# Reordering the first and the last stage of a one-core attention block kernel: load order, parking, interleaved broadcasts, double-buffered weights and row sums on two engines

## The chip, the cores and the metric

The kernel runs on one core of a Trainium2 chip. The metric is the device time of one execution in microseconds (us); the lower, the better. Runs of the kernel before, on the same chip, go with every group of runs, because the chips differ by a little over 0.1% for one and the same kernel.

In the profile PE is TensorE (matmul), DVE is VectorE, ACT is ScalarE, POOL is GpSimd, SP is SyncE. A load or store lands when its last bytes have been moved. The granted clock is the share of TensorE's full clock that the profile shows as granted. A line such as `1800.43 8.15 DVE L642 TENSOR_TENSOR wq_sb<-wq_sb,bc_t 128x15360 ...` reads: start in us, busy us, engine, source line, operation, output and inputs, their shapes, how many are put together (x2), and in square brackets how long the engine stood idle before it and what released it.

## The reference, cut to what matters

A decode step of a transformer block whose normalisation is modulated by a conditioning vector `c`; the kernel returns the output and the gradients of nine inputs.

```python
mod = (silu(c) @ w_mod).reshape(1, 6, 1, 640)          # w_mod: 640 x 3840
sa, ca, ga, sb, cb, gb = mod[:, 0], ..., mod[:, 5]
h = layernorm(x) * (1 + ca) + sa                       # 1 x 640
q = h @ wq                                             # wq: 640 x 6144, 32 heads of 192
o = softmax(q k^T * 192 ** -0.5) v                     # k, v cache: 32 heads x 8192 x 192
x = x + ga * (o @ wo)
...                                                    # MLP, modulated by sb, cb, gb
# outputs: x, and by the chain rule d_x, d_k, d_v, d_wq, d_wo, ..., d_c, d_w_mod
```

What matters for the tail, given the gradient `dq` (6144 numbers): `d_wq = h^T dq` (an outer product, 640 x 6144), `d_h = dq @ wq^T` (row sums of `wq * dq`), and from `d_h` the gradient `d_mod` (3840 numbers); then `d_w_mod = silu(c)^T d_mod` and `d_silu = d_mod @ w_mod^T` in the same two forms.

## The kernel before: the parts that the change touches

Helpers: `row_to_col` turns a row on one partition into columns, by one small fp32 matmul for each 128 elements; `park` keeps such columns in memory for the end; `col_to_row` and `unpark` turn them back, also by matmuls and copies by ACT; `vecmat` multiplies a column vector with a weight matrix in chunks of 512; `bcast_row` spreads a row over 128 partitions by a matmul with ones and a copy.

The head, before the first key block is used:

```python
    x0 = load_row(A_x[0], D, "x0")
    c_row = load_row(c, D, "c_row")
    # ... silu(c) -> sc, sc_col_f, sc_col_bf
    wmod_sb = w0.tile([P, NDC, NMOD], BF16, name="wmod_sb")
    nc.sync.dma_start(out=wmod_sb, in_=w_mod.rearrange("(i p) n -> p i n", p=P))
    wq_sb = w0.tile([P, NDC, QD], BF16, name="wq_sb")
    nc.gpsimd.dma_start(out=wq_sb, in_=A_wq.rearrange("(i p) n -> p i n", p=P))

    vecmat(sc_col_bf, NDC, wmod_sb, NMOD, mod_row, chunk=480)
    # ... layernorm -> n0; h_a -> ha_col_f, ha_col_bf
    vecmat(ha_col_bf, NDC, wq_sb, QD, qs_row_bf, chunk=512, scale=SCALE)
    bcast_row(qs_row_bf, QD, qs_bc, copy_eng="scalar")
    x0_c = park(x0, NDC, "x0_c")
    c_c = park(c_row, NDC, "c_c")
    sig_c = park(sig, NDC, "sig_c")
    mod_c = park(mod_row[0:1, D : 6 * D], 5 * NDC, "mod_c")
    n0_c = park(n0, NDC, "n0_c")
```

Then come the forward attention, the output projection and the MLP with their gradients, and the backward attention, which ends with `dq_col_f`. None of this changes. The tail:

```python
    nc.vector.tensor_copy(out=dq_col_f, in_=dqcol_ps)
    # ...
        wmod_sb2 = fin.tile([P, NDC, NMOD], BF16, name="wmod_sb2")
        nc.sync.dma_start(out=wmod_sb2, in_=w_mod.rearrange("(i p) n -> p i n", p=P))
        col_to_row(dq_col_f, NQC, dq_row_bf)                       # all 48 columns
        for half in range(2):
            hs = slice(half * QH, (half + 1) * QH)
            wq_sb2 = fin.tile([P, NDC, QH], BF16, name="wq_sb2", tag="wqh")   # one buffer
            nc.sync.dma_start(out=wq_sb2, in_=wq_v[:, :, hs])
            # ... dq_bc = this half of dq, on all partitions
            nc.vector.tensor_tensor(out=wq_sb2, in0=wq_sb2, in1=dq_bc[:, None, :].to_broadcast([P, NDC, QH]), op=ALU.mult)
            # dha_c, or dha_c2 and a sum for half 1:
            nc.vector.reduce_sum(out=dha_c, in_=wq_sb2, axis=AX.X)
            for i in range(NDC):                                   # staged outer product, two buffers
                stg = fino.tile([P, NMOD], BF16, name="stg", tag="stg")
                nc.vector.tensor_scalar(out=stg[:, 0:QH], in0=dq_bc, scalar1=ha_col_f[:, i : i + 1], scalar2=None, op0=ALU.mult)
                nc.gpsimd.dma_start(out=out_4[i * P : (i + 1) * P, hs], in_=stg[:, 0:QH])
        d_ha = unpark(dha_c, NDC, "d_ha")
        n0 = unpark(n0_c, NDC, "n0r")
        # ... car, d_x1, sig, c_row, and four col_to_row into d_mod: nine steps in all
        # ... d_mod complete, layernorm backward, d_x
        # ... dmod_bc = d_mod on all partitions, in one go
        nc.vector.tensor_tensor(out=wmod_sb2, in0=wmod_sb2, in1=dmod_bc[:, None, :].to_broadcast([P, NDC, NMOD]), op=ALU.mult)
        nc.vector.reduce_sum(out=dsc_c, in_=wmod_sb2, axis=AX.X)
        # ... five staged outer products into out_9; unpark(dsc_c); d_c; store
```

## Time and profile before

| what | kernel before |
|---|---|
| time, median of the first 4 runs (lowest to highest) | 1945.89 us (1944.86 to 1947.25) |
| modulation weights landed, first product on PE | 30.21 us |
| query products start | 58.07 us |
| first K product on DVE | 79.67 us |
| copy of dq_col | 1753.06 us |
| last dK store landed | 1768.0 us |
| end of the span | 1944.0 us |

The windows view of the kernel before, one line a stage: head, forward attention, MLP and projections, backward attention, tail. After the length come the busy us of each engine with its instructions in brackets, then the granted TensorE clock, the busy share of the DMA engines, and what they moved.

```profile
core 0: us, PE busy (x) PEld busy (x) DVE busy (x) ACT busy (x) POOL busy (x), PEclk, DMA share, GB/s
0.00:80.00 80.00, 50.24 (x222) 30.13 (x222) 6.64 (x21) 25.20 (x44) 2.13 (x10) 0.86 0.49 199
80.00:640.00 560.00, 289.41 (x2339) 238.17 (x2340) 451.99 (x354) 224.16 (x1186) 2.22 (x1) 0.69 0.93 369
640.00:815.00 175.00, 98.12 (x485) 54.26 (x483) 67.08 (x141) 39.84 (x80) 19.48 (x26) 0.64 0.63 181
815.00:1753.00 938.00, 279.81 (x2176) 226.27 (x2176) 882.20 (x2492) 688.86 (x2013) 67.14 (x126) 0.63 0.99 420
1753.00:1944.00 191.00, 40.48 (x226) 20.60 (x226) 105.49 (x38) 27.67 (x60) 10.96 (x19) 0.58 0.41 163
```

The two attention stages have the DMA engines busy for 93% and 99% of the time (in the second, DVE is busy for 882 of 938 us too). The change takes no work out of them; it is meant to let them start earlier, and e1 below tests whether they hand that on. In the head (first line) and the tail (last line) no engine is near 100%: there one thing waits for the next, and these 271 us are what the change works on.

The timeline of PE in the head of the kernel before:

```profile
30.21 9.98 PE L173 MATMUL vm_ps<-wmod_sb,sc_col_bf 128*1 128x480 bf16 x40 [20.92 <-DMA wmod_sb<-in_w_mod_dram]
...
45.21 10.80 PE L161 MATMUL col_ps<-ones_row_f,mod_row 1*128 1x1 f32 x50
55.87 2.27 PE L161 MATMUL col_ps<-ones_row_f,ln_n 1*128 1x1 f32 x10
58.07 14.55 PE L173 MATMUL vm_ps<-wq_sb,ha_col_bf 128*1 128x512 bf16 x60
```

and of DVE, the first K product:

```profile
79.67 6.63 DVE L320 TENSOR_TENSOR prod<-K_sb,qs_bc 128x6144 bf16<-128x6144 bf16 x2 [21.33 <-PE bc_ps L150]
```

PE stands idle for 20.92 us until the modulation weights are there. Then 10.80 us of parking stand ahead of the query products, although in the source the parks are written after them: what is written last need not run last. The products are followed by twelve broadcasts, and the first key product on DVE comes at 79.67.

The chain of waits at the start of the tail of the kernel before (start, us, what):

```profile
1754.06 13.95 DMA out_dram<-dK
1768.46 0.58 ACT dq_row_bf L120
1769.09 11.54 PE c2r_ps L118 x80
```

The last dK store takes 13.95 us to land; only then does the chain go on, because the memory of the tail's tiles is the one that the stores still read. Then 48 columns are turned to rows (11.54 us) before the first broadcast.

The timeline of DVE in the same tail:

```profile
1784.31 1.95 DVE L651 TENSOR_SCALAR stg<-bc_t,ha_col_f 128x3072 bf16<-128x3072 bf16 x2 [31.04 <-ACT bc_t L152]
1794.52 1.02 DVE L651 TENSOR_SCALAR stg<-bc_t,ha_col_f 128x3072 bf16<-128x3072 bf16 x1 [8.26 <-DMA out_dram<-stg]
...
1800.43 8.15 DVE L642 TENSOR_TENSOR wq_sb<-wq_sb,bc_t 128x15360 bf16<-128x15360 bf16 x1
1808.62 16.15 DVE L644 TENSOR_REDUCE dha_c<-wq_sb 128x5 f32<-128x15360 bf16 x1
...
1835.82 1.02 DVE L651 TENSOR_SCALAR stg<-bc_t,ha_col_f 128x3072 bf16<-128x3072 bf16 x1 [9.19 <-DMA out_dram<-stg]
...
1844.06 8.15 DVE L642 TENSOR_TENSOR wq_sb<-wq_sb,bc_t 128x15360 bf16<-128x15360 bf16 x1
1852.25 16.16 DVE L647 TENSOR_REDUCE dha_c<-wq_sb 128x5 f32<-128x15360 bf16 x1
...
1906.00 20.15 DVE L678 TENSOR_REDUCE dsc_c<-wmod_sb 128x5 f32<-128x19200 bf16 x1
```

All five staged products run ahead of each multiply, and with two buffers the third waits until the first has been stored (8.26 and 9.19 us). A reduction takes twice as long as the multiply before it. The waits view sums the waits for staged stores up (engine and line, waited for what, us in all, times, longest):

```profile
DVE stg L651 <- DMA out_dram<-stg: 25.7, 6, 9.2
DVE stg L681 <- DMA out_dram<-stg: 2.9, 2, 1.8
```

That is 28.6 us in 8 waits. Not all of it lengthens the chain: with one buffer the load of the second half is issued 71.7 us after the dq_col copy and lands at 88.1, so the second multiply, at 91.0, could have come at most 2.9 us earlier without any wait for a store.

### The profile page before, as it was taken

Reading aid. Unit: us, or ns where it says so; the run is one execution under the profiler, and the core shown is the slowest. Engines: PE = TensorE matmul, PEld = TensorE weight load, DVE = VectorE, ACT = ScalarE, POOL = GpSimd, SP = SyncE. Lnnn points to the kernel's source line nnn. Section 1 sums busy time; section 2 is a strip of 40 time slices with the busy share of each in tenths; the row PEclk is TensorE's granted clock in tenths of the full one; section 3 lists DMA queues with packets and bytes.
Section 4 is the critical chain, followed back from the end, with each engine's and each line's share of the span. In section 5 each row is a group of like instructions: output and inputs, shape, how many; then the busy total and the mean of one; then the engine's idle time right before and its main releaser. Section 6 shows DMA issues by size and latency. Waiting matters only on the chain. (4 is left out here: it accounts for less than half of the span.)

```text
span 1944.0 us, 18733 instructions
## 1 busy us (share of the span) xinstructions
PE 758.0 (39%) x5447; PEld 569.4 (29%) x5447; DVE 1513.4 (78%) x3043; ACT 1005.7 (52%) x3379; POOL 101.9 (5%) x181
## 2 busy tenths in 40 slices
PE   4644555555554754433223233232232232333030
PEld 2333444444444433222222122122122121232010
DVE  1268888888888153499899999999999999991667
ACT  2424434444344211576677777776776777782020
POOL 0000000000000011100000000000000000010000
PEclk9667777676677755666566566666665666666565
DMA  6599999999996528999999999999999999979402
GB/s 263 198 402 417 377 379 372 381 372 379 383 380 271 139 65 204 343 385 429 429 429 429 428 427 429 429 429 429 429 428 427 424 426 427 426 314 370 194 5 101
DMA packets 112621, 678.93 MB, mean 349 GB/s; under 512 B 53764, under 2 KB 53767, under 8 KB 62727
## 3 DMA queue, kind: packets, MB, share of 16 engines
q1 hardware_dynamic: 86278, 432.17, 56.1%
q0 software_dynamic: 26240, 245.58, 30.1%
q8 instruction: 42, 0.69, 0.1%
q14 instruction: 61, 0.49, 0.1%
HBM read 440.01 MB, written 225.91 MB: 343 GB/s over the span
## 5 line engine op out<-in xcount | busy, mean ns | idle before, releaser
L594 PE MATMUL dq_ps<-K_sb,dS_bf 128*1 128x192 bf16 x2048 | 257.7, 304 | 570.7 <-ACT dS_bf L580 570.7
L601 ACT ACTIVATE dK<-qs_bc,dS 128x192 bf16<-128x192 bf16 x960 | 355.4, 440 | 169.3 <-DMA out_dram<-dK 154.3
L600 ACT ACTIVATE dV<-do_bc,P_all 128x192 bf16<-128x192 bf16 x960 | 355.4, 440 | 81.1 <-DMA out_dram<-dV 75.4
L594 PEld LDWEIGHTS <-dS_bf 128*1 128x1 bf16 x2048 | 207.4, 104 | 615.8 <-ACT dS_bf L580 582.5
L603 DVE TENSOR_SCALAR dV<-do_bc,P_all 128x192 bf16<-128x192 bf16 x1088 | 285.3, 262 | 8.6 <-DMA out_dram<-dwo_sb 8.5
L323 ACT ACTIVATE junk<-prod 128x192 bf16<-128x192 bf16 x512 | 178.0, 349 | 216.8 <-DVE prod L320 216.8
L604 DVE TENSOR_SCALAR dK<-qs_bc,dS 128x192 bf16<-128x192 bf16 x1088 | 284.9, 262 | 0.0
L570 DVE TENSOR_TENSOR bprod<-V_sb,do_bc 128x6144 bf16<-128x6144 bf16 x64 | 214.8, 3357 | 55.8 <-DMA V_sb<-in_A_v_cache_dram 55.8
L320 DVE TENSOR_TENSOR prod<-K_sb,qs_bc 128x6144 bf16<-128x6144 bf16 x64 | 213.7, 3340 | 39.6 <-PE bc_ps L150 21.3
L353 PE MATMUL o_ps<-V_sb,E_all 128*1 128x192 bf16 x2048 | 238.3, 294 | 0.0
L353 PEld LDWEIGHTS <-E_all 128*1 128x1 bf16 x2048 | 203.1, 101 | 28.1
L572 DVE TENSOR_TENSOR bh<-bprod 128x3072 bf16<-128x3072 bf16 x64 | 112.0, 1750 | 0.0
L576 DVE TENSOR_REDUCE dP<-bh 128x32 f32<-128x1536 bf16 x64 | 111.7, 1745 | 0.0
L323 ACT ACTIVATION_READ_ACCUMULATOR junk<-prod 128x1 f32 x512 | 95.6, 187 | 0.0
L336 PE MATMUL m1T<-ident_f,m 128*1 128x128 f32 x32 | 11.9, 372 | 208.8 <-DVE m L334 208.8
L326 DVE TENSOR_TENSOR h<-prod 128x2304 bf16<-128x2304 bf16 x64 | 86.9, 1358 | 2.1
L329 DVE TENSOR_REDUCE S_h<-h 128x24 f32<-128x1152 bf16 x64 | 86.6, 1353 | 2.2
L605 POOL DMA_DIRECT2D out_dram<-dV x64 | 34.2, 534 | 881.3 <-DVE dK L604 513.1
L336 PEld LDWEIGHTS m1T<-ident_f,m 128*1 128x1 f32 x32 | 2.5, 79 | 212.4 <-DVE m L334 197.4
L574 DVE TENSOR_TENSOR bh<-bh 128x1536 bf16<-128x1536 bf16 x64 | 60.8, 950 | 0.0
L651 DVE TENSOR_SCALAR stg<-bc_t,ha_col_f 128x3072 bf16<-128x3072 bf16 x10 | 10.0, 1018 | 56.7 <-ACT bc_t L152 31.0
L328 DVE TENSOR_TENSOR h<-h 128x1152 bf16<-128x1152 bf16 x64 | 48.5, 758 | 2.2
(300 smaller groups left out, 856.7 us busy)
## 6 DMA issues: line engine op xcount, KB each, us to landing
K_sb<-in_A_k_cache_dram SPq DMA_DIRECT2D x128, 1536.0 KB, 12.8
V_sb<-in_A_v_cache_dram SPq DMA_DIRECT2D x128, 1536.0 KB, 12.7
out_dram<-dV POOLq DMA_DIRECT2D x64, 1536.0 KB, 17.0
out_dram<-dK POOLq DMA_DIRECT2D x64, 1536.0 KB, 23.8
wmod_sb<-in_w_mod_dram SPq DMA_DIRECT2D x2, 4800.0 KB, 21.7
wq_sb<-in_A_wq_dram POOLq DMA_DIRECT2D x1, 7680.0 KB, 32.6
wo_sb<-in_A_wo_dram POOLq DMA_DIRECT2D x1, 7680.0 KB, 69.2
out_dram<-dwo_sb POOLq DMA_DIRECT2D x12, 640.0 KB, 6.4
```

Source lines behind the costliest of these rows:

```text
L320: nc.vector.tensor_tensor(out=prod, in0=K_sb, in1=qh[:, None, :].to_broadcast([P, JH, DH]), op=ALU.mult)
L323: nc.scalar.activation(out=junk, in_=prod[:, jj, :], func=ACT.Copy, accum_out=S_h[:, t * JH + jj : t * JH + jj + 1])
L326: nc.vector.tensor_tensor(out=h1, in0=prod[:, JACC_F:JH, 0 : DH // 2], in1=prod[:, JACC_F:JH, DH // 2 : DH], op=ALU.add)
L353: nc.tensor.matmul(o_ps, lhsT=E_all[:, h, j : j + 1], rhs=V_halves[t][:, jj, :], start=(j == 0), stop=(j == J - 1))
L570: nc.vector.tensor_tensor(out=prod, in0=V_sb, in1=doh[:, None, :].to_broadcast([P, JH, DH]), op=ALU.mult)
L572: nc.vector.tensor_tensor(out=h1, in0=prod[:, :, 0 : DH // 2], in1=prod[:, :, DH // 2 : DH], op=ALU.add)
L576: nc.vector.reduce_sum(out=dP, in_=h2, axis=AX.X)
L594: nc.tensor.matmul(dq_ps, lhsT=dS_bf[:, jj : jj + 1], rhs=K_sb[:, jj, :], start=(j == 0), stop=(j == J - 1))
L600: nc.scalar.activation(out=dV[:, jj, :], in_=doh, func=ACT.Copy, scale=P_all[:, h, j : j + 1])
L601: nc.scalar.activation(out=dK[:, jj, :], in_=qh, func=ACT.Copy, scale=dS[:, jj : jj + 1])
L603: nc.vector.tensor_scalar(out=dV[:, jj, :], in0=doh, scalar1=P_all[:, h, j : j + 1], scalar2=None, op0=ALU.mult)
L604: nc.vector.tensor_scalar(out=dK[:, jj, :], in0=qh, scalar1=dS[:, jj : jj + 1], scalar2=None, op0=ALU.mult)
```

## The change

Its intent: in the head, have the modulation weights land first, park early what is known early, and mix broadcasts into the query products. In the tail, load both halves of the query weights at once into two buffers, do the nine column-to-row steps while the last stores land, make `dq_bc` in chunks straight from the columns, put multiply and row sums ahead of most staged products, and give three of five row sums to ACT. The diff, cut to its core:

```diff
+    def vecmat_bcast(col_bf, nk, W_sb, N, row_bf, out_bc, scale=None):
+        # ... as vecmat, but after the products of one chunk the broadcast of the
+        #     chunk before it; its copies go to DVE and ACT in turn
...
+    x0_c = park(x0, NDC, "x0_c")
+    c_c = park(c_row, NDC, "c_c")
     sig = new_row(D, name="sig")
     nc.scalar.activation(out=sig, in_=c_row, func=ACT.Sigmoid)
+    sig_c = park(sig, NDC, "sig_c")
...
-    nc.gpsimd.dma_start(out=wq_sb, in_=A_wq.rearrange("(i p) n -> p i n", p=P))
+    nc.sync.dma_start(out=wq_sb, in_=A_wq.rearrange("(i p) n -> p i n", p=P))
...
+    mod_c = park(mod_row[0:1, D : 6 * D], 5 * NDC, "mod_c")
...
-    vecmat(ha_col_bf, NDC, wq_sb, QD, qs_row_bf, chunk=512, scale=SCALE)
-    bcast_row(qs_row_bf, QD, qs_bc, copy_eng="scalar")
-    # ... the five parks
+    vecmat_bcast(ha_col_bf, NDC, wq_sb, QD, qs_row_bf, qs_bc, scale=SCALE)
...
+        for half in range(2):
+            wq_sb2 = fin2.tile([P, NDC, QH], BF16, name="wq_sb2", tag="wqh")      # two buffers
+            nc.sync.dma_start(out=wq_sb2, in_=wq_v[:, :, half * QH : (half + 1) * QH])
+            wq_halves.append(wq_sb2)
+        for half in range(2):
+            if half == 0:
+                wm_sb2 = fin.tile([P, NDC, MH], BF16, name="wm_sb2", tag="wmh")
+            else:
+                wm_sb2 = fin2.tile([P, NDC, MH], BF16, name="wm_sb2", tag="wqh")
+            nc.sync.dma_start(out=wm_sb2, in_=wm_v[:, :, half * MH : (half + 1) * MH])
+            wm_halves.append(wm_sb2)
         n0 = unpark(n0_c, NDC, "n0r")
         # ... the other eight column-to-row steps, now ahead of all else
+        NACC = 3
+        def rowsums(prod3, nrows, ncolsn, out_col):
+            for i in range(min(NACC, nrows)):
+                nc.scalar.activation(out=prod3[:, i, :], in_=prod3[:, i, :], func=ACT.Copy, accum_out=out_col[:, i : i + 1])
+            if nrows > NACC:
+                nc.vector.reduce_sum(out=out_col[:, NACC:nrows], in_=prod3[:, NACC:nrows, :], axis=AX.X)
...
+        for half in range(2):
+            dq_bc = fin2.tile([P, QH], BF16, name="dq_bc", tag="bct2")
+            for g in range(QH // 512):
+                # ... four columns to a row chunk (rowc), its broadcast, into dq_bc
+            wqh = wq_halves[half]
+            nc.vector.tensor_tensor(out=wqh, in0=wqh, in1=dq_bc[:, None, :].to_broadcast([P, NDC, QH]), op=ALU.mult)
+            rowsums(wqh, NDC, QH, dha_c if half == 0 else dha_c2)
+            for i in range(NDC):
+                # ... staged outer products as before
...
+        # dmod_bc in chunks of 480; staged products of out_9; then for each half of w_mod:
+            nc.vector.tensor_tensor(out=wmh, in0=wmh, in1=dmod_bc[:, None, half * MH : (half + 1) * MH].to_broadcast([P, NDC, MH]), op=ALU.mult)
+            rowsums(wmh, NDC, MH, dsc_c if half == 0 else dsc_c2)
```

## The prediction

> **What bounds the kernel now.** By the busy table in slices, DMA is at 90% or more in the forward (85 to 600 us) and backward (760 to 1768) attention, at 380 to 429 GB/s. The change touches neither; it touches the head (0 to 79.7 us) and the tail (1753 to 1944), where one chain runs and DMA is mostly idle.
>
> *Head.* By the timeline the modulation weights land at 30.2 us, sharing the DMA engines with the query weights on the other queue. Their products take 10 us. Then 50 column matmuls for parking (45.1 to 55.9) and other parks stand ahead of the query products, which start at 58.07 though their weights were there by about 34. Products take 14.6 us, then twelve broadcasts 7 us on one engine; the first K product starts at 79.67.
>
> *Tail.* The chain of waits starts with the last dK store landing at 1768.0, then: twelve column-to-row groups and six broadcasts (to 1784.3), five staged outer products held by their stores, a 128x15360 multiply (8.15 us) and its reduction (16.15), the last three twice; nine column-to-row steps (1871 to 1887.5); eight broadcasts; a 19200 multiply (10.16), its reduction (20.15), and an end of 18 us.
>
> **The change, costed.**
>
> 1. Both head weights on one queue: modulation weights land at about 16 (the tail's load of the same 4800 KB took 14.6 us with another behind it), query weights still at about 34.
> 2. Parks of x, c and sigmoid move into the initial wait. The modulation park stays before h_a: 26 + 12.5 = 38.5 for the query products (was 58.1). Products interleaved with broadcasts, evacuated by two engines: 18.5 us, so the first K product at 57. Saving 22 us; the forward stage shifts whole.
> 3. The nine column-to-row steps move into the wait for the last stores (1753 to 1768). Half the modulation weights load there too, delaying those stores by up to 6 us (2.4 MB at 429 GB/s), to about 1773.
> 4. Column-to-row and broadcast go in pairs; the first half is ready at about 1782. Query weights land about 1785.
> 5. Two staged products precede each multiply, not five, so DVE hardly waits for stores.
> 6. Of each reduction DVE keeps 2 of 5 rows (16.15 x 2/5 = 6.5 us), ACT takes 3. The Trainium skill, "VectorE: DVE Perf Modes", perf-mode tier table, gives tensor_reduce only the 1x mode and bf16 tensor_tensor 2x; the trace agrees (1.05 against 0.53 ns an element). For ACT, "ScalarE: Activation LUTs", What ACT_TABLE_LOAD costs, gives 186 ns + 0.833 ns an element: estimate 2.75 us a row of 3072, 8.6 for three; 192-element rows took 349 ns in this trace, which agrees.
>
> Estimated tail: first multiply 1785 to 1793, second 1802 to 1811, dha complete 1820 (was 1868.6), modulation broadcast complete 1835 (was 1894.8), last multiply ends 1853, dsc 1860 (was 1926), end 1870 (was 1944). Saving 74 us, all on the chain.
>
> **Predicted:** 1850 us, 8 in 10 within 1838 to 1864. Faster by over 2%: 0.98; within 2%: 0.015; slower: 0.005.
>
> **What shows it.** First K product at 55 to 60; forward and backward durations unchanged within 5 us; from dq_col to the end 117 us (was 191); ACT row sums of 2.5 to 3 us; DVE waits for staged stores below 8 us in total (was 28.6).
>
> **What would make it wrong.** The two head loads interleave, so modulation weights land late; forward gives the head back; prefetch delays the last stores more than 6 us; ACT row sums above 3.2 us; small row casts on DVE lengthening the broadcast chain.

## The result, and the profile after

| | before | after |
|---|---|---|
| time, median | 1945.67 us (12 runs, 1943.98 to 1949.44) | 1847.53 us (8 runs, 1840.93 to 1850.4) |
| ratio, 95% interval | | 0.949 [0.948, 0.9501] |

A ratio is the mean time of one kernel's fast runs over that of the other's of the same rounds, so it is not quite the ratio of the medians quoted here. The difference of the medians is 98.1 us. The execution that was profiled is the fastest of the eight (1840.93 us); a second profile of the same kernel, below as e9_after_again, shows where it was lucky.

| landmark (us) | before | after | predicted |
|---|---|---|---|
| first product of the modulation weights | 30.21 | 16.01 | about 16 |
| query products start | 58.07 | 37.91 | 38.5 |
| first K product | 79.67 | 57.93 | 57 |
| dq_col copy to the landing of the last dK store | 15.0 | 18.5 | up to 20 |
| dq_col copy to the first multiply | 47.4 | 30.8 | 32 to 40 |
| dq_col copy to dha complete | 115.4 | 66.1 | 67 |
| dq_col copy to the broadcast of d_mod complete | 141.7 | 80.3 | 82 |
| dq_col copy to the end | 190.9 | 114.8 | 117 |

The predicted tail positions are those of the prediction less 1753. The head is 79.67 - 57.93 = 21.7 us shorter and the tail 190.9 - 114.8 = 76.1 us: 97.9 us in all, close to the difference of the medians (98.1 us).

The windows view of the kernel after, the same five stages with their new borders:

```profile
0.00:58.00 58.00, 49.88 (x222) 28.75 (x222) 9.96 (x27) 21.54 (x38) 1.07 (x8) 0.91 0.68 275
58.00:619.00 561.00, 291.50 (x2338) 240.32 (x2338) 452.28 (x354) 224.49 (x1186) 2.38 (x1) 0.69 0.93 368
619.00:785.00 166.00, 94.47 (x487) 52.16 (x487) 66.87 (x139) 38.43 (x77) 19.34 (x26) 0.68 0.62 180
785.00:1724.00 939.00, 285.25 (x2176) 229.49 (x2176) 882.49 (x2495) 689.60 (x2015) 67.13 (x126) 0.63 0.99 421
1724.00:1839.00 115.00, 37.07 (x226) 18.56 (x226) 74.24 (x49) 55.21 (x84) 11.58 (x19) 0.65 0.68 271
```

Forward and backward attention take 561 and 939 us where they took 560 and 938: they gave nothing and took nothing back. In the tail DVE has 74.24 us of work instead of 105.49, ACT 55.21 instead of 27.67: that is the row sums moving over. In the third stage this execution is 9 us shorter than the kernel before; nothing of the change is in that stage, and its clock happened to be 0.68 against 0.64.

The timeline of PE in the head of the kernel after:

```profile
16.01 10.71 PE L200 MATMUL vm_ps<-wmod_sb,sc_col_bf 128*1 128x480 bf16 x40 [4.54 <-DMA wmod_sb<-in_w_mod_dram]
26.65 4.96 PE L188 MATMUL col_ps<-ones_row_f,mod_row 1*128 1x1 f32 x42
...
37.91 4.07 PE L121 MATMUL vb_ps<-wq_sb,ha_col_bf 128*1 128x512 bf16 x10 [0.33 <-DVE ha_col_bf L191]
41.91 0.38 PE L110 MATMUL vb_bps<-qs_row_bf,ones_row_bf 1*128 1x512 bf16 x1
42.22 1.24 PE L121 MATMUL vb_ps<-wq_sb,ha_col_bf 128*1 128x512 bf16 x5
```

and of DVE, the first K product:

```profile
57.93 3.36 DVE L346 TENSOR_TENSOR prod<-K_sb,qs_bc 128x6144 bf16<-128x6144 bf16 x1
```

From 16.01 to the first K product at 57.93 PE is busy for 41.2 of 41.9 us; products and broadcasts alternate (1.24 and 0.38 us). The head was waiting for memory and now follows PE, although the 50 parking matmuls in it hide behind the load of the query weights, which lands at 35.2.

The chain of waits at the start of the tail of the kernel after:

```profile
1725.17 17.55 DMA out_dram<-dK
1742.85 12.07 DMA wq_sb<-in_A_wq_dram
1754.94 7.93 DVE wq_sb L708
```

The last store now needs 17.55 us, 3.6 more than before, because half of the modulation weights is loaded beside it. The row conversion has left the chain; the load of the first query half has taken its place.

The timeline of DVE in the tail of the kernel after, and below it the waits view for staged stores:

```profile
1751.76 1.95 DVE L712 TENSOR_SCALAR stg<-dq_bc,ha_col_f 128x3072 bf16<-128x3072 bf16 x2 [15.85 <-ACT dq_bc L706]
1754.94 8.16 DVE L708 TENSOR_TENSOR wq_sb<-wq_sb,dq_bc 128x15360 bf16<-128x15360 bf16 x1 [1.23 <-DMA wq_sb<-in_A_wq_dram]
1763.02 1.01 DVE L712 TENSOR_SCALAR stg<-dq_bc,ha_col_f 128x3072 bf16<-128x3072 bf16 x1
1763.95 6.55 DVE L691 TENSOR_REDUCE dha_c<-wq_sb 128x2 f32<-128x6144 bf16 x1
...
1772.27 8.15 DVE L708 TENSOR_TENSOR wq_sb<-wq_sb,dq_bc 128x15360 bf16<-128x15360 bf16 x1
...
1810.42 4.13 DVE L691 TENSOR_REDUCE dsc_c<-wm_sb 128x2 f32<-128x3840 bf16 x1
```

```profile
DVE stg L712 <- DMA out_dram<-stg: 0.6, 1, 0.6
```

From the first multiply to dha complete DVE is busy for 34.7 of 35.4 us: 17.3 us from the first multiply to the second instead of 43.6, and 0.6 us of waiting for stores instead of 28.6. The timeline of ACT shows the row sums that it took over:

```profile
1763.13 2.76 ACT L689 ACTIVATE wq_sb<-wq_sb 128x3072 bf16<-128x3072 bf16 x1 [3.90 <-DVE wq_sb L708]
1765.81 0.19 ACT L689 ACTIVATION_READ_ACCUMULATOR wq_sb<-wq_sb 128x1 f32 x1
```

### The profile page after: what moved, and what is told of

Read it like the earlier page. It is cut to its first block, busy times and chain, and to the rows that moved or that the text cites. A ratio compares the mean times of both kernels' runs of the same rounds, so it can differ in the third digit from the quotient of the medians.

```text
span 1839.0 us, 18782 instructions
## 1 busy us (share of the span) xinstructions
PE 758.2 (41%) x5447; PEld 569.3 (31%) x5447; DVE 1485.8 (81%) x3059; ACT 1029.3 (56%) x3397; POOL 101.5 (6%) x180
## 3 DMA queue, kind: packets, MB, share of 16 engines
q0 software_dynamic: 25584, 237.71, 30.8%
## 4 chain that ended last, share of the span: by engine, by line
DMA 46%; DVE 38%; PE 8%; issue 4%; ACT 2%; SPq 1%; POOL 0%; DVEq 0%; POOLq 0%
DMA V_sb<-in_A_v_cache_dram 39%; DVE prod L346 11%; DVE bprod L596 7%; DVE h L352 4%; DVE S_h L355 4%; DMA K_sb<-in_A_k_cache_dram 3%; PE vm_ps L200 3%; DVE h L354 2%; DVE dK L630 2%; DVE dV L629 1%; PE col_ps L188 1%; SPq L516 1%; DMA out_dram<-dK 1%; PE negm_ps L368 1%; DVE bh L598 1%
## 5 line engine op out<-in xcount | busy, mean ns | idle before, releaser
L620 PE MATMUL dq_ps<-K_sb,dS_bf 128*1 128x192 bf16 x2048 | 263.9, 310 | 567.1 <-ACT dS_bf L606 567.1
L620 PEld LDWEIGHTS <-dS_bf 128*1 128x1 bf16 x2048 | 211.4, 106 | 614.4 <-ACT dS_bf L606 578.9
L630 DVE TENSOR_SCALAR dK<-qs_bc,dS 128x192 bf16<-128x192 bf16 x1088 | 288.7, 266 | 0.0
L375 DVE RECIPROCAL rinv_all<-tot_ps 1x1 f32<-1x1 f32 x32 | 5.0, 155 | 56.4 <-PE tot_ps L374 56.4
```

Source lines behind the costliest of these rows:

```text
L620: nc.tensor.matmul(dq_ps, lhsT=dS_bf[:, jj : jj + 1], rhs=K_sb[:, jj, :], start=(j == 0), stop=(j == J - 1))
L630: nc.vector.tensor_scalar(out=dK[:, jj, :], in0=qh, scalar1=dS[:, jj : jj + 1], scalar2=None, op0=ALU.mult)
```

## The experiments

The main theory: the gain is the sum of a head that is shorter because the weights of the first product land first, and a tail that is shorter because DVE, its limit, does less (row sums) and waits less (second buffer, order). Most parts were undone or done alone; the order of the staged products and the making of `dq_bc` in chunks straight from the columns were not. Twelve runs were made, e9 with the changed kernel itself; all gave correct results. "Tail" below is the time from the dq_col copy to the end, read from the profile; it is free of what the middle of the program does, which moves by several us from run to run.

### One half of the change at a time: e1_head_only and e2_tail_only

Edit: e1 has the head of after and the tail of before; e2 the reverse.

```diff
 # e1_head_only: the change, less everything from the line
-    with tc.tile_pool(name="fin", bufs=1) as fin, tc.tile_pool(name="fin2", bufs=2) as fin2:
+    with tc.tile_pool(name="fin", bufs=1) as fin, tc.tile_pool(name="fino", bufs=2) as fino:
 # ... to the end, which is that of the kernel before; e2_tail_only: the other half
```

> The head of the changed kernel with the tail of the kernel before. Theory (head and tail are two separate chains that add, with DMA-bound stages between that only shift): first K product at 57.9 us as in the changed kernel, from the dq column copy to the end 191 us as before, total 1945.7 - 21.7 = 1924 us (within 3). Rival (the forward stage is bound by DMA, so a head that ends early only waits for data and gives the time back): within 3 us of before, 1943 or more.

Measured: 1922.86 us (1919.67 to 1928.19), ratio 0.9885 [0.9863, 0.9907]; first K product at 58.5, tail 190.4 us. The gain is clear of noise, though below the 2% from which a verdict is "faster".

> The head of the kernel before with the tail of the changed kernel. Theory: first K product at 79.7, from the dq column copy to the end 115 us, total 1945.7 - 76 = 1869.6 us (within 3). Rival (head and tail share something, such as memory layout or queue state, and do not add): more than 6 us off that.

Measured: 1871.72 us (1870.61 to 1878.37), ratio 0.9626 [0.9608, 0.9645]; first K product at 80.0, tail 115.3 us.

Against the 1945.88 us of before on the same chip these are 23.0 and 74.2 us, 97.2 us together, against 98.1 for the whole change. Both theories hold. The two halves add up: neither needs the other, and the attention stages between them hand the head's gain on in full.

### The head: e3_queue_back and e4_serial_qs

Edit of e3, only the queue of one load:

```diff
-    nc.sync.dma_start(out=wq_sb, in_=A_wq.rearrange("(i p) n -> p i n", p=P))
+    nc.gpsimd.dma_start(out=wq_sb, in_=A_wq.rearrange("(i p) n -> p i n", p=P))
```

> The changed kernel with only the query weights' load put back on the other queue; the order on every engine is otherwise the same. Theory (the shared queue serves the modulation weights first and so starts the tensor engine's chain 14 us earlier): modulation weights land at 30 us again instead of 16, first K product at 57.9 + 14.2 = 72, total 1847.5 + 14 = 1861.5 us. Rival (the engines are the same 16 and the last byte of both loads lands at 35 us either way; the moved parks made the head's gain): first K product at 58 to 61, total within 3 us of 1847.5.

Measured: 1861.03 us (1855.17 to 1866.65), ratio 0.9564 [0.9541, 0.9587]. The first product of the modulation weights starts at 29.99 instead of 16.01, the first K product at 72.06 instead of 57.93. Both move by 14 us. So 14 of the head's 21.7 us come from one word: with the two loads on two queues the first one needed shares the DMA engines with the second, on one queue it does not. The Trainium skill, "DMA: Bandwidth & Descriptors", section "Queues, rings and completion order", says that each DMA engine goes round between the queues that have work and takes each queue's own descriptors in order; this trace agrees (14.5 us from issue to landing for the modulation weights with the other load behind them in the same queue, 28.5 in e3 with it on the other queue).

Edit of e4, products first and broadcasts after them, as in before:

```diff
-    vecmat_bcast(ha_col_bf, NDC, wq_sb, QD, qs_row_bf, qs_bc, scale=SCALE)
+    vecmat(ha_col_bf, NDC, wq_sb, QD, qs_row_bf, chunk=512, scale=SCALE)
+    bcast_row(qs_row_bf, QD, qs_bc, copy_eng="scalar")
```

> The changed kernel with the twelve query products and twelve broadcasts one after the other, as before, all evacuated by ACT. My prediction costed the interleaving as 21.6 us to 18.5; the changed trace shows 20.0 us. Theory (PE is the bound of both forms, so only what it did not do meanwhile is won): the stretch from the first query product to the first K product is 21.6 us, total 1847.5 + 1.6 = 1849 us. Rival (the 7 us of broadcasts were hidden whole): plus 7 us, 1854.5.

Measured: 1850.63 us (1850.08 to 1853.31), ratio 0.9514 [0.9499, 0.9528]; first K product at 59.98, 2.05 us later than in after. By the time alone (3.1 us above the median of after, which ran on another chip) the two expectations are hard to tell apart; the landmark decides for the small figure. The head of after stands in nine more traces, with the first K product at 57.3 to 58.5; against all ten the interleaving brings 1.4 to 2.7 us, some 2 us. The rest of the head (21.7 - 14.1 - 2.1 = 5.5 us, or about that) is the parking that moved into the first wait or behind the load of the query weights; that remainder was worked out, not run.

### The row sums: e5_no_act_sums

```diff
-        NACC = 3
+        NACC = 0
```

> The changed kernel with all row sums on VectorE again. Theory (VectorE is the limit from the first multiply to the end, so the row sums taken by ScalarE come off one for one): in the trace of after, three rows of 3072 elements cost VectorE 9.6 us (two took 6.55) and three rows of 1920 cost 5.94 us (two took 4.13), two halves of each: 9.6 x 2 + 5.94 x 2 = +31 us, about 1878.5 us, range 1873 to 1883; ScalarE nearly idle after dq_col. Rival (the sums ran in the shade of the loads and of the stores, and the gain is that of the prefetch): under +10 us, below 1858.

Measured: 1880.21 us (1873.49 to 1881.1), ratio 0.9638 [0.9605, 0.9671]. The tail is 146.7 us instead of 114.8: 31.9 us longer, where 31.1 were expected from the durations of rows. The reduction of five rows takes 16.15 us again instead of 6.55. The rival falls: what ACT takes over comes off the tail one for one, as it should where DVE is the limit. Of the tail's 76.1 us this part is 32.

### The second buffer: e8_wq_single

```diff
-            wq_sb2 = fin2.tile([P, NDC, QH], BF16, name="wq_sb2", tag="wqh")
+            wq_sb2 = fin.tile([P, NDC, QH], BF16, name="wq_sb2", tag="wq1")
 # ... and the second half of the modulation weights in the same single buffer
```

> The changed kernel with one buffer for both halves of the query weights, as in before, so that the second half is loaded only once the row sums of the first are done; the order of all instructions stays. Theory (the early load into a second buffer is needed, the order alone is not enough): the second multiply comes 12 to 18 us later than in after, and the end 9 to 14 us later: about 1859 us. Rival (the order of the queue alone did it, because stores no longer stand ahead of the load): within 4 us of after, below 1852.

Measured: 1862.7 us (1858.18 to 1863.77), ratio 0.9555 [0.953, 0.9581]. The second multiply starts 66.7 us after the dq_col copy instead of 48.1 (18.6 later, a little above the 12 to 18 expected), and the tail is 130.1 us, 15.3 longer (9 to 14 expected). The waits view of e8_wq_single shows what came back:

```profile
DVE stg L712 <- DMA out_dram<-stg: 16.2, 4, 9.4
```

With one buffer the second load starts only when the row sums of the first half are done. It lands 62.4 us after the copy. DVE has nothing else to do in the meantime, so four staged products of the second half run ahead of the second multiply (after has none there) and wait for each other's stores, which share the DMA engines with the load. The order in the source is that of after; what puts the waits back is the late load. One thing besides the buffer moved: the first modulation half, which after issues 0.5 us after the copy, beside the last stores, is issued at 15.6 here, and the first multiply comes at 29.0 instead of 30.8. So the 15.3 us are not of the second buffer alone; what this shift does by itself was not run.

### Which load runs beside the last stores: e6_wm_late

```diff
-                wm_sb2 = fin.tile([P, NDC, MH], BF16, name="wm_sb2", tag="wmh")
+                wm_sb2 = fin2.tile([P, NDC, MH], BF16, name="wm_sb2", tag="wqh")
```

> The changed kernel, with the first half of the modulation weights in a buffer of the query-weight halves, so that it is loaded only after the first row sums; nothing else moves. Theory (this half, 1.97 MB, is loaded while the last dV and dK stores land and delays them by 3.6 us: 17.55 us from issue to landing against 13.95 in before): the stores land 14 us after issue, the tail is 3 to 4 us shorter, about 1844 us. Rival (the stores are not what the tail waits for, or the query-weight halves delay them just as much): within 1 us of after, 1847.

Measured: 1852.94 us (1851.22 to 1860.19), ratio 0.9517 [0.9487, 0.9546]; the tail is 118.6 us, 3.8 longer, not 3 to 4 shorter. Both expectations missed. (The text has 1.97 MB for the half; it is 640 x 1920 x 2 bytes, 2.46 MB.) The first step holds: the last store needs 14.2 us again, and the first multiply starts 28.7 us after the dq_col copy instead of 30.8, the second at 46.4 instead of 48.1. But then the timeline of DVE of e6_wm_late has this line, which after does not have:

```profile
1805.90 1.02 DVE L712 TENSOR_SCALAR stg<-dq_bc,ha_col_f 128x3072 bf16<-128x3072 bf16 x1 [5.31 <-DMA out_dram<-stg]
```

Gone from beside the dK stores, the load comes later, and now one of the two modulation halves is loaded 63.0 to 75.9 us after the copy, where after has no load, beside the staged stores, and DVE waits 5.31 us for one of them. The DMA view shows it: in the 11 us from 1795 on the load moves 2.23 MB and the stores 1.23, and the staged stores issued there take 10.4 us to land in the median; at the same place of after (from 1787 on) there is no load, the stores move 2.26 MB, and take 3.8 us. The bytes have to be moved somewhere. Beside the dK stores they cost about 2 us at the first multiply; later they cost more than 5. The prediction counted the early load only as a cost; against the place where it would otherwise go, it is a gain.

### The column-to-row steps: e7_unpark_late

```diff
-        n0 = unpark(n0_c, NDC, "n0r")
-        # ... and the eight others
 ...
         d_ha = unpark(dha_c, NDC, "d_ha")
+        n0 = unpark(n0_c, NDC, "n0r")
+        # ... and the eight others
```

> The changed kernel with the nine column-to-row steps back behind d_ha, where before has them. Theory (placed early they ran while the last stores landed; placed late their first five stand between d_ha and d_n0, and hide only partly): +5 to +10 us, about 1854 us, with the first multiply no later than in after. Rival one: they come back in full, +15 us or more, 1862 or above. Rival two (they are hidden wherever they stand): within 2 us of after.

Measured: 1855.52 us (1851.64 to 1856.79), ratio 0.952 [0.9495, 0.9545]; the tail is 123.1 us, 8.3 longer. The theory holds. The first staged product comes 29.2 us after the dq_col copy, where after has 27.6: taking the nine steps out of the way of the broadcast does not let it start earlier, since ACT's first copy of it then waits 18.27 us for the landing of the dK store. In after the steps end 16.8 us and the landing 18.5 us after the copy, side by side: taking away one of the two leaves the other. Undone singly, row sums, second buffer and these steps come to 31.9 + 15.3 + 8.3 = 55.5 of the tail's 76.1 us; the rest was not taken apart, and parts undone singly need not add up.

### The changed kernel again: e9_after_again

The same text; no diff.

> The changed kernel again, not a word different, for its profile and as the yardstick of the next run on the same chip. If the profiled run of after (1840.9 us where its seven other runs took 1846 to 1850) was merely lucky in the middle of the program, then this one's head (first K product at 57.9 us) and tail (114.8 us from the dq_col copy to the end) agree within 1.5 us with it, the dq_col copy comes at 1730 to 1734 instead of 1724.2, and the median is 1844 to 1851. If head or tail differ by more, then the sum -21.7 - 76.1 rests on a single lucky trace.

Measured: 1849.49 us (1842.37 to 1852.11), ratio 0.9488 [0.947, 0.9507]. First K product at 58.18, dq_col copy at 1733.5, tail 114.8 us. Head and tail repeat within 0.3 us, and the middle is 1675.3 us here, 1666.3 in the first profile of after, 1673.4 in before. So the first profile was lucky in the middle, and the accounting of head and tail does not hang on it.

### Trying to start the first multiply earlier: e11_early_tail, e12_one_load_first, e13_whole_rows

In after DVE still idles 15.85 us before the first staged product. e7 says that two things must go at once: the steps ahead of the broadcast, and the memory that the last stores still read.

```diff
 # e11_early_tail
+    fin2_cm = tc.tile_pool(name="fin2", bufs=2)     # opened first: its memory is not that of the dK and dV tiles
+    fin2 = fin2_cm.__enter__()
...
+        for half in range(2):
+            dq_bc = fin2.tile([P, NMOD], BF16, name="dq_bc", tag="bct2")
+            # ... both halves of dq_bc are made first; then three column-to-row steps, then d_mod's four;
+            #     the last two only at the end
```

> The changed kernel with the broadcast of dq ahead of the column-to-row steps, and with the query-weight halves, the broadcast, the staging tiles and three of the rows in memory that the last dV and dK tiles do not use. Theory (in after both the column-to-row steps on TensorE and ScalarE, 17 us, and the landing of the last stores, 17.55 us from issue, stand ahead of the broadcast, so that the first multiply starts 30.8 us after the dq_col copy; take both away and only the load of the first half is left, which shares the memory bandwidth with the last stores): first multiply 19 to 23 us after the dq_col copy, dha complete at 55 to 60 instead of 66.1, the tail 101 to 109 us instead of 114.8; 6 to 14 us faster than after on the same chip, about 1837 us. Rival (VectorE then waits for the staged stores, which queue behind the last dK stores): the multiply starts early but the second one does not, and the gain is under 4 us.

Measured: 1846.35 us (1840.29 to 1849.76), ratio 0.9468 [0.9449, 0.9487], beside e9_after_again on the same chip: 3.1 us less by the medians, but the intervals overlap, so the times alone do not tell the two apart. The tail is 113.3 us, 1.5 shorter. The theory fails in its main figure: the first multiply starts 29.9 us after the copy, not 19 to 23. The broadcast is indeed ready 12 us after it, but the load is not. The rival has the size of the gain right (under 4 us) but not the reason: DVE has no wait for a staged store at all. The waits view of e11_early_tail:

```profile
DVE wq_sb L718 <- DMA wq_sb<-in_A_wq_dram: 15.9, 1, 15.9
DVE stg L722 <- ACT dq_bc L694: 11.8, 1, 11.8
```

One explanation was that the two query halves, issued together, hold each other up.

```diff
 # e12_one_load_first: as e11, and for half 1 (the modulation loads follow it, issued 21.8 us after the copy; 22.1 in e11)
+                nc.vector.tensor_copy(out=wq_halves[1][:, 0, 0:1], in_=dq_bc[:, QH - 1 : QH])
+                nc.sync.dma_start(out=wq_halves[1], in_=wq_v[:, :, QH : 2 * QH])
```

> The early tail, with the load of the second query half held back until the broadcast of the first half of dq is done (a one-column copy into its buffer, overwritten by the load, makes it wait), so that the first half does not share the queue with it. Theory (in the early tail the first half came only 29.6 us after its issue because it moved side by side with the second one, which nobody needs before; alone beside the last stores it needs 18 to 21 us): first multiply 18 to 21 us after the dq_col copy, second at 36 to 40, tail 103 to 107 us, 7 to 11 us faster than the changed kernel, a ratio of 0.943 to 0.9455 to before. Rival (the stores take the bandwidth first and the load gets it only once they have landed): the first half lands 24 us or later, and the tail is at best 4 us shorter than 114.8 us.

Measured: 1846.63 us (1845.84 to 1854.23), ratio 0.9484 [0.9457, 0.9511]; first multiply 29.7 us after the copy, tail 113.1 us. The theory falls: holding the second load back by 11 us changes nothing for the first. The rival's figures hold, with a landing after 24 us and a tail less than 4 us shorter: what holds the load up is the other queue. The DMA view of e12_one_load_first in the 15 us from 1732 on, when the load was issued (packets, MB, share of the 16 engines; q0 has the stores, q1 the loads):

```profile
q0 software_dynamic: 406, 4.40, 75.2%
q1 hardware_dynamic: 259, 1.59, 25.3%
```

The stores get 4.40 MB through, the load 1.59: they do not go wholly first, as the rival has it, but they get most. A packet of the stores has 12288 bytes here (48 of the 406 are of under 512 bytes and set aside), one of the load 6144 (half a row of the weights). If the queues take turns by packets, longer packets should give the load a larger share. So the last run splits the weights by rows instead of columns:

```diff
 # e13_whole_rows: as e11, but
+        for i0, i1 in ((0, 3), (3, 5)):
+            wq_sb2 = fin4.tile([P, i1 - i0, QD], BF16, name="wq_sb2", tag=f"wq{i0}")
+            nc.sync.dma_start(out=wq_sb2, in_=wq_v[:, i0:i1, :])
 # ... one multiply a part; ACT sums rows 0, 1 and 3, DVE rows 2 and 4; staged products after each
```

> The early tail, with the query weights split by rows instead of columns: three of the five row blocks first (4.72 MB), then two, so that each packet of the load is a whole row of 12288 bytes, as long as those of the dK and dV stores, instead of a half row of 6144; multiply, row sums and staged stores follow this split, with the same work in all (VectorE 13.1 us of row sums, ScalarE three rows of 6144). Theory (the two queues take turns by packets, so that the bytes of each go with its packet length: in the early tail with one load first the stores moved 4.40 MB and the load 1.59 MB in the first 15 us of the load): packets of equal length let the load have about half, the first part lands 21 to 25 us after the dq_col copy although it is 0.8 MB larger, the first multiply (9.8 us long) starts then, the tail is 103 to 108 us, 7 to 12 us faster than the changed kernel, a ratio of 0.943 to 0.9455. Rival (the stores come first whatever the packets are): landing at 29 us or later, tail 112 us or more, a ratio of 0.948 or above.

Measured: 1841.46 us (1837.68 to 1844.01), ratio 0.9455 [0.9428, 0.9481]; the tail is 109.5 us, 5.3 shorter than in after. In the 15 us from 1733 on the stores move 3.71 MB and the load 2.31: its share rose from 27% (1.59 of 5.99 MB) to 38% (2.31 of 6.02). But both stretches begin with some 4 us in which no packet of the load has started (e12: issued at 1731.8, none before 1736.2). The same view of the 12 us after that, from 6 to 18 us after the copy, first e12_one_load_first, then e13_whole_rows:

```profile
q0 software_dynamic: 296, 3.24, 65.6%
q1 hardware_dynamic: 296, 1.82, 36.2%
```

```profile
q1 hardware_dynamic: 225, 2.76, 54.1%
q0 software_dynamic: 221, 2.33, 45.8%
```

Of q0's packets 32 and 31 have under 512 bytes. That leaves 264 packets of the stores beside 296 of the load in e12, and 190 beside 225 in e13: about one for one, whatever their length. The load's share of the bytes is 36% and 54%. So the theory's turn by packets is what the traces show, and the load got its half; the rival falls. The staged stores play no part in it: their rows have 6144 bytes, and by the view q0 has no packet of that length in these stretches yet.

The figures were still missed: the first multiply starts 28.1 us after the copy, not 21 to 25. The first 4 us without a packet are part of that, since the expectation counted none; the rest was not worked out. Of the 5.3 us, 2.7 are there at the first multiply and 4.7 where d_ha is first used (64.4 us after the copy instead of 69.1); the rest comes later. How much of the 5.3 us is the packet length, and how much the new split into three and two rows, was not separated.

e13 is the fastest kernel here, by its time and by its tail. Its interval overlaps that of after narrowly (0.9481 against 0.948), and the two did not run on the same chip, so "about 5 us faster than after" rests on the tail of one profile and on the ratios 0.9455 and 0.949.

## Why the prediction was right

The time, 1850 us, was 2.5 us above the median measured; the sum came out for the reasons given: the head gave 21.7 us where 22 were predicted, the tail 76.1 where 74 were. Point by point:

1. *Both head weights on one queue.* Predicted: landing at about 16. Measured: 16.01, and e3 shows that this step alone is 14 us.
2. *Query products at 38.5.* Measured: 37.91. The parks of x, c and sigmoid did move into the first wait.
3. *Products interleaved with broadcasts, 18.5 us.* This term was mis-sized: it is 20.0 us (37.91 to 57.93), and 19.7 to 21.0 in the ten traces with this head. The prediction does not say what its 18.5 were made of; over the 14.6 of products that it cites they leave 3.9 for the broadcasts and the last copy. The traces show more: with a broadcast in between, five products come every 1.49 us, without it (e4) every 1.08, so twelve broadcasts take 4.9 us of PE. What goes along with the differences between the traces is a slow start after the parking. The windows view of the kernel after (the columns as above; the clock is the number after the busy times):

```profile
37.90:41.90 4.00, 3.99 (x10) 1.09 (x10) 0.00 (x0) 0.59 (x1) 0.00 (x0) 0.55 0.83 273
41.90:57.90 16.00, 15.63 (x63) 4.36 (x62) 4.15 (x6) 8.77 (x16) 0.00 (x0) 1.00 0.30 128
```

   The first ten products take 4.07 us; at the pace of the later ones (1.24 us for five) they would take 2.5. That does not explain the miss, since the kernel before starts slowly too (3.0 us at a clock of 0.50, within the 14.6). The clock falls during the parking: from 31.7 to 37.9 it is 0.50, although PE counts as busy for 5.9 of these 6.2 us with small matmuls of that kind. The Trainium skill, "TensorE: Matmul & The Clock Gate", section "What's actually happening", says that the array is throttled by default and let go after some 3.4 us of sustained work; the trace of after agrees (3.4 us of slow products), the others with this head show 2.9 to 5.7 us. e4 shows that the interleaving is worth only about 2 us.
4. *Forward and backward unchanged.* 561 against 560 and 939 against 938 us; e1 and e2 add up to the whole.
5. *The prefetch delays the stores by up to 6 us.* Mis-sized as well: 3.6 us (17.55 against 13.95). The upper bound took the whole 2.4 MB at the full rate as delay; the stores were done before the load was, and e6, without it, has 14.2. e6 also shows what the prediction did not see: that the place beside the dK stores is cheaper for this load than the one after them.
6. *First multiply 32 to 40 us after the copy.* Measured 30.8, since the stores landed earlier than feared. From there to dha complete 35.4 us (27 to 35 predicted), to the broadcast of d_mod 14.2 (15), to the end 34.5 (35).
7. *DVE hardly waits for stores.* 0.6 us against a bound of 8. e8 shows that this needs the second buffer.
8. *Of each reduction DVE keeps two rows; ACT needs 2.75 us a row.* Measured 6.55 us (6.5) and 2.75 to 2.76 us (2.75), plus 0.19 us to read the sum out, and 8.35 us for three in a row (8.6); e5 puts 31.9 us on it. The Trainium skill, "VectorE: DVE Perf Modes", section "The perf-mode tier table (the rule you actually need)", gives tensor_reduce only the 1x mode, and the trace agrees: 16.15 us for 15360 elements, 1.05 ns each, against 0.53 ns for the multiply. The Trainium skill, "ScalarE: Activation LUTs", section "What ACT_TABLE_LOAD costs", gives 186 ns + 0.833 ns an element; that is 2.745 us for 3072 elements, as measured, and 1.785 for 1920, where the trace has 1.78 to 1.80.

What the prediction left out: that the nine early column-to-row steps take 17 us themselves and end just when the stores have landed (e7), so that they are hidden by luck of size (the prediction's own figures are 16.5 us for them and 15 for the wait that they move into); and that the first query half, not the stores, becomes the next limit of the tail (e11 to e13).

## What to carry to other kernels

When two loads are issued at the start and one is needed first, put them on one queue in that order: it was 14 us here for one word. In a serial tail, first find the engine that is busy from the first to the last step (here DVE), give part of its slowest operation to an idle engine, and check which buffers its loads wait for: with a single buffer the order in the source did not hold, and the tail was 15 us longer. Before moving a load out of a crowded stretch, ask what it will meet in the next one: the delayed load of e6 cost more there than it had cost before.

## What the Trainium skill lacked or had wrong

- "ScalarE: Activation LUTs" gives the cost of an activation (186 ns + 0.833 ns an element, confirmed here), but not the extra instruction that reads a row sum out: 0.18 to 0.19 us after each of the 2.75 us sums.
- "DMA: Bandwidth & Descriptors", section "Queues, rings and completion order", says that an engine changes between queues at packet granularity, but not what shares of the bytes two queues get. Measured with dK and dV stores of 12288 bytes a packet on one queue and a weight load on the other, once both moved data (packets as the profile counts them, those under 512 bytes left out): 255 to 288 with 3840-byte rows of the load (after, 6 to 16 us after the dq_col copy), 264 to 296 with 6144 (e12) and 190 to 225 with 12288 (e13). About one for one each time, so the load's share of the bytes was 26%, 36% and 54%.
  What it meant for the load: 29 us from issue to landing for 3.93 MB beside the last stores (e12), where the modulation weights of the head (4.92 MB) took 14.5 us with no store beside them.
